# Order of the DMA queue and of three engine steps in the opening rounds of a linear-attention and expert kernel

## The chip, the cores and the metric

The kernel runs on one core of a Trainium2 chip. The metric is the device time of one execution in microseconds (us). A core has TensorE (matrix products), VectorE, ScalarE, GpSimd (POOL in the profile) and SyncE (SP), which here only issues transfers. Each engine runs its own queue of instructions in the order in which the program gives them, and an instruction that waits holds back all that is queued behind it on its engine. A transfer is issued by an engine's queue (nearly all of those below by SyncE's) and then runs on the core's 16 DMA engines.

## The reference

A linear attention with a decaying state feeds a mixture of experts whose gate is normalised over tokens and experts:

```python
# B=4, H=8, S=768, D=48; x has B*S = 3072 rows of H*D = 384; E = 8 experts, F = 1024
for t in range(S):
    cur = u * k[t] (outer) v[t]
    y[t] = r[t] @ (state + cur)
    state = w * state + k[t] (outer) v[t]
x = y as [3072, 384]
P = exp(x @ w_gate - max);  8 times: normalise rows, then columns
out = sum over e of P[:, e] * (relu(x @ w1[e]) @ w2[e])
```

All tensors are float32.

## The kernel before

**Tiles and rounds.** The 3072 tokens are 24 tiles of 128. The front of the kernel is a loop over rounds `i` (lines 791 to 850), software-pipelined over the tiles by a hand-written order: round `i` prepares tile `i+2`, turns tile `i+1`, forms the attention products of tile `i`, finishes the output of tile `i-1`, sends tile `i-2` through a transposing DMA and forms the gate logits of tile `i-3`. Expert 0's products are placed between these steps as units of work (`work`), from round 3 on; before that `work` issues three products of zeros as filler (`spin`, output `pz`). Behind the front, the other seven experts are computed in half-expert stages with a product scheme that uses combined tokens; this part is not changed.

**The steps**, each with the names under which the profile shows it:

- `load_part(tt, nm, src)` (line 314) loads r, k or v of a tile on SyncE (`rn`, `kn`, `vn`; tile 3's r and k go to a part of `hb`, those of tiles 4 and 5 to parts of `xv`). There are five buffers for v: tile `i+4` takes that of tile `i-1`. There are three buffers for r and k.
- `prep(tt)` (526): POOL multiplies r by a decay table (`rp`), VectorE does k (`kp`).
- `bonus_dot` and `bonus` (532, 541): POOL forms `rk` from r, k and u, VectorE reduces it to `dg`, POOL multiplies it into v and adds a term (`rk<-vn,dg`, `rk<-rk,hbx`).
- `stage_b(tt)` (551), the turn: eight TensorE transposes by products with the identity (`prT`, `pkT`), and ScalarE copies them out of PSUM (`rT`, `kT`).
- `stage_c(tt)` (562): the A products r by k (`pA`, 32 small matmuls), VectorE's masked copy (`at`), the state's products (`pu`), VectorE's and POOL's update of the state (`S`).
- `stage_d(tt)` (606): the output products (`py`), which are the last readers of the tile's v; VectorE sums (`x`), finds the largest value (`xm`) and a power-of-two scale (`inv_s`, `xs`).
- `scale_x(tt)` (639): ScalarE writes the high float16 part of the scaled x (`xsc`), VectorE the low part (also `xsc`).
- `stage_e(tt)` (646): SyncE issues the transposing DMA `hbx<-xsc`. Expert 0's products on this tile (`pht`, or `ph` from tile 3 on) and its gate logits (`px`, `stage_f`) read its result.
- `gate_across`, `gate_split` (511, 516): the scale and float16 split of the gate's weights (`pmax_wg`, `iswg`, `wgp`).

The PSUM pool of the attention products (`pa`) has four banks, taken in turn by prT, pkT, two of pA, pu and py.

**Expert 0's weights** are split into float16 high and low parts in small steps: `split_weights` (151) makes a list for w1 and then w2, each of three maxima on VectorE (`wm`), their maximum (`wma`), the maximum over partitions through TensorE (`pmax_w`), the scale (`isw`, `sw`), the high part's first half on ScalarE, the high part's second half with the low part's first half, and the low part's second half on VectorE (`ws`). `steps(n)` takes the next `n` of the list. How many each round takes, before and after `stage_d`, is the table `STEPS` (773). Two steps are taken ahead of the loop, three in round 0, so that round 1's two are w1's scale and the first half of its high part. The first `pht` product of round 3 needs w1's first halves, the first `po` product of round 6 those of w2.

**The order in the queues.** In rounds 2 to 19 the program issues r, k and v of tile `i+4` at the start of the round, and then `scale_x` and `stage_e` of tile `i-2`. In round 1, `stage_b(2)` comes ahead of `stage_c(1)`. Partial outputs of expert 0 are stored by SyncE too (`e0d<-stg`), and tokens of the later stages are copied by it (`xv<-hbx`).

Of the kernel before, what the change touches and what calls it, by code (L numbers as in the profile page):

```python
# [32 lines left out]
def rwkv_sinkhorn_moe(  # L33
# [24 lines left out]
    NTT = NT // P  # L58
# [27 lines left out]
    def part(home, dtype, at, shape):  # L86

        n = 1
        for s_ in shape:
            n *= s_  # L90
        x_ = home if home.dtype == dtype else home.bitcast(dtype)
        x_ = x_[:, at : at + n]
        if len(shape) == 1:
            return x_
        names = "abcd"[: len(shape)]
        return x_.rearrange(
            f"p ({' '.join(names)}) -> p {' '.join(names)}", **{c_: s_ for c_, s_ in zip(names[1:], shape[1:])}
        )
# [29 lines left out]
    def pow2_scale(m, inv, s, down):  # L128
        V.tensor_scalar(inv, m, 1e-30, down, op0=ALU.max, op1=ALU.mult)
        V.tensor_single_scalar(  # L130
            inv.bitcast(I32), inv.bitcast(I32), EXP_MASK, op=ALU.bitwise_and
        )
        V.reciprocal(s, inv)
# [144 lines left out]
    def whole(gen):  # L278
        leave()
        for _ in gen:  # L280
            pass
# [23 lines left out]
    def spin(n):  # L305
        pz = ps2.tile([P, TB], F32, tag="po", name="pz")
        for _ in range(n):
            T.matmul(pz, zeros[:, :P], zeros, start=True, stop=True)
# [5 lines left out]
    def load_part(tt, nm, src):  # L314
        b, c = divmod(tt, NCHB)
        if tt == 3 and nm != "v":
            t_ = part(hb3, F32, HB + "rk".index(nm) * H * D, (H, D))
        elif tt in (4, 5) and nm != "v":
            t_ = part(xv0_, F32, (2 * tt - 8 + "rk".index(nm)) * H * D, (H, D))
        else:  # L320
            t_ = ld.tile([P, H, D], F32, tag=nm + "n", name=f"{nm}n_{tt}", bufs=5 if nm == "v" else 3)
        Q.dma_start(t_, src[b, :, c * C : (c + 1) * C, :].rearrange("h t d -> t h d"))
        loads.setdefault(tt, {})[nm] = t_

    def load_chunk(tt):
        for nm, src in (("r", r), ("k", k), ("v", v)):
            load_part(tt, nm, src)
# [180 lines left out]
    def gate_max():  # L508
        V.tensor_reduce(wgm, wg, axis=AX.XY, op=ALU.max, apply_absolute_value=True)
# [16 lines left out]
    def prep(tt):  # L526
        ld_ = loads[tt]
        G.tensor_tensor(rp_[tt % 2][:, :, :D], ld_["r"], rt4, op=ALU.mult)
        V.tensor_tensor(kp_[tt % 3][:, :, :D], ld_["k"], kt4, op=ALU.mult)
        st[tt] = {}  # L530
# [20 lines left out]
    def stage_b(tt):  # L551
        d = st[tt]
        for nm, src in (("rT", rp_[tt % 2]), ("kT", kp_[tt % 3])):
            pt = ps3.tile([P, NPAIR, P], F32, tag="pa", name=f"p{nm}_{tt}")
            sv = src.rearrange("p (a j) d -> p a (j d)", j=2)
            for p_ in range(NPAIR):
                T.transpose(pt[:, p_, :], sv[:, p_, :], ident)
            dst = at2.tile([P, NPAIR, P], F32, tag=nm, name=f"{nm}_{tt}", bufs=3 if nm == "rT" else 2)
            S_.copy(dst, pt)
            d[nm] = dst  # L560
# [45 lines left out]
    def stage_d(tt):  # L606
        d = st[tt]
        c = tt % NCHB
        vn = loads[tt]["v"]
        at = at_[tt % 2]  # L610
        py = ps3.tile([P, H, D], F32, tag="pa", name=f"py_{tt}")
        pyp = py.rearrange("p (a j) d -> p a (j d)", j=2)

        halves = [slice(i * HP, (i + 1) * HP) for i in range(2)]
        first = True
        if c > 0:
            for p_ in range(NPAIR):
                for hs in halves:
                    T.matmul(
                        pyp[hs, p_, :], d["rT"][:, p_, hs], d["S"][:, p_].rearrange("p j d -> p (j d)"),  # L620
                        start=first, stop=False, skip_group_check=True,
                    )
                first = False
        for h in range(H):
            for hs in halves:
                T.matmul(
                    py[hs, h, :], at[:, h, hs], vn[:, h, :],
                    start=first, stop=(h == H - 1), skip_group_check=True,
                )
            first = False  # L630
        x = at2.tile([P, DM], F32, tag="x", name=f"x_{tt}")
        V.tensor_tensor(x, py.rearrange("p h d -> p (h d)"), d["av"].rearrange("p h d -> p (h d)"), op=ALU.add)
        m = at2.tile([P, 1], F32, tag="xm", name=f"xm_{tt}")
        V.tensor_reduce(m, x, axis=AX.X, op=ALU.max, apply_absolute_value=True)
        s = at2.tile([P, 1], F32, tag="xs", name=f"xs_{tt}")
        pow2_scale(m, inv_s[:, tt : tt + 1], s, 0.125)
        d["x"], d["s"] = x, s
# [97 lines left out]
    def token_steps(parts, sums=False):  # L735

        rebuild, singles, pool, high, low = parts
        steps = [[lambda th=th: rebuild(th)] for th in range(TH)]
        steps += [[f] for f in pool]
        if sums:  # L740
            return [lambda fs=fs: [f() for f in fs] for fs in steps]
        steps[2].append(singles)
        steps += [[], [], [], []]
        for (i, n), at_ in zip(PARTS, (5, 11, 15, 19)):
            steps[TH + at_].append(lambda i=i, n=n: high(i, n))
            steps[TH + at_ + 1].append(lambda i=i, n=n: low(i, n))
        return [lambda fs=fs: [f() for f in fs] for fs in steps]
# [6 lines left out]
    def prepare():  # L754
        if side and need.get(id(side[0]), 0) <= emitted[0]:
            side.pop(0)()

    def work(n, ready=True):
        if not ready:
            spin(3)  # L760
            return
        for _ in range(n):
            if units:
                whole(units.pop(0))
# [3 lines left out]
    for sg in range(3):  # L768
        steps = token_steps(early[sg], sg == 2)
# [1 line left out]
        side += steps  # L771

    STEPS = {
        0: (3, 0), 1: (0, 2), 2: (1, 1), 3: (2, 1), 4: (1, 0), 5: (1, 3), 6: (1, 0), 7: (0, 0), 8: (0, 0),
    }
    FIRST = TH

    def n_steps(i):
        return STEPS.get(i, (2, 2) if i < 22 else (3, 2))

    def steps(n):
        for _ in range(n):
            prepare()
# [7 lines left out]
    for i in range(NTT + 3):  # L791
        if i == 1:
            gate_max()
        if i + 2 < NTT:
            if i == 1:
                load_part(5, "v", v)
            elif 1 < i < NTT - 4:
                load_chunk(i + 4)
            if i:
                prep(i + 2)  # L800
        if i + 1 < NTT:
            bonus_dot(i + 1)
        if i + 1 < NTT and i:
            stage_b(i + 1)
        if 2 <= i <= NTT + 1:
            scale_x(i - 2)
            stage_e(i - 2)
            emitted[0] = i - 1
        work(1, i >= FIRST)
        if i < NTT:  # L810
            if i:
                bonus(i)
            if ("S", i) in st:
                st[i]["S"] = st.pop(("S", i))
            stage_c(i)
        if i == 0:
            fill(at_[1].rearrange("p h c -> p (h c)"))
            bonus(0)
            prep(2)
        if i == 2:  # L820
            gate_split(gate_res)
        if i == 0:
            stage_b(1)
        if i <= NTT:
            work(2 if i > 11 else 1, i >= FIRST)
        if i == 1:
            gate_res = gate_across()
        if i >= 3:
            bank_ = ps2.tile([P, TB], F32, tag="po", name=f"px_{i}")
        if i > NTT:  # L830
            work(2)
        steps(n_steps(i)[0])
        leave()
        if 1 <= i <= NTT:
            stage_d(i - 1)
        steps(n_steps(i)[1])
        if 3 <= i:
            stage_f(i - 3, bank_)
        done = i - 2
        if 0 <= done < TH:  # L840
            units += [g1_tile(done, j, W) for j in range(2)]
        if done == TH - 1:
            units += [g2_half(0, t, j, W) for j in range(2) for t in range(TH)]
        if TH <= done < NTT and done % TH == TH - 1:
            po_ = done // TH
            for j in range(2):
                g1 = [g1_unit(po_, fc, W) for fc in range(j * FHC, (j + 1) * FHC)]
                g2 = [g2_half(*a, W) for a in pend]
                units += merged(g1, g2)
                pend = [(po_, t, j) for t in range(TH)]  # L850
# [402 lines left out]
    for s in range(NS):  # L1253
        tasks = stage_tasks(s)
        for g in range(NG):
            for j in range(2):
                for n, nxt in enumerate(g1_slots(s, g, j)):
# [3 lines left out]
                    i = j * NPR + n  # L1261
# [37 lines left out]
```

## Time and profile before

| | |
|---|---|
| median of 3 runs | 1552.06 us (1550.48 to 1552.35) |
| profiled execution, own time | 1552.62 us |
| its span | 1551.1 us |
| TensorE busy | 1522.5 us, 98% |
| VectorE busy | 1026.8 us, 66% |
| ScalarE busy | 663.0 us, 43% |
| POOL busy | 596.2 us, 38% |
| front, rounds 0 to 26 | about the first 262 us |
| granted TensorE clock, mean | 0.993 |

Busy shares are means over stages with different limits, so the opening is read from the timeline, where each row has a start, a duration, the engine, the operation, its output and inputs, and in brackets the idle time of that engine just before, with what ended it. "SPq" is SyncE's queue: its rows are the issuing of a transfer, not the transfer. A busy TensorE is one whose pipeline holds products, at whatever clock; the granted clock is in the windows.

### The profile page before, as it was taken

What the parts mean: (1) busy time and instruction counts of PE and PEld (TensorE: products, weight loads), DVE (VectorE), ACT (ScalarE), POOL (GpSimd) and SP (SyncE); (2) the same over time, 40 slices, a digit from 0 to 9 for tenths busy, and PEclk for the clock granted to TensorE, in tenths of its full rate; (3) what the DMA queues carried; (4) which work ended last, traced back from release to release, by engine and by line L of the source; (5) the groups of instructions that cost most, each with busy time, mean ns of one, the idle gap of its engine ahead of it and who ended that gap; (6) DMA issues with size and microseconds to landing.
All of it is one profiled execution on the core that took longest, in us unless ns stands there. A gap on an engine that the chain in (4) does not pass through costs nothing.

```text
span 1551.1 us, 26486 instructions
## 1 busy us (share of the span) xinstructions
PE 1522.5 (98%) x10441; PEld 866.5 (56%) x10441; DVE 1026.8 (66%) x1715; ACT 663.0 (43%) x1164; POOL 596.2 (38%) x712
## 2 busy tenths in 40 slices
PE   7899999999999999999999999999999999999999
PEld 4766776555555555555555555555555555555555
DVE  7778885867665666766666666656566666656554
ACT  4233333524444453545444454535454444535320
POOL 7558995520202424242433424242423324242200
PEclk9899999999999999999999999999999999999999
DMA  8355533121226566576667566655545555545434
GB/s 193 61 113 108 127 83 104 49 77 50 97 58 109 73 122 95 72 124 93 126 87 129 79 122 90 124 69 86 65 59 97 60 97 60 97 56 100 54 90 134
DMA packets 186848, 143.14 MB, mean 92 GB/s; under 512 B 109537, under 2 KB 180961, under 8 KB 186721
## 3 DMA queue, kind: packets, MB, share of 16 engines
q0 software_dynamic: 44928, 61.36, 32.1%
q1 hardware_dynamic: 141584, 80.07, 18.8%
q8 instruction: 82, 1.34, 0.4%
q14 instruction: 46, 0.37, 0.1%
q10 hardware_dynamic: 208, 0.00, 0.0%
HBM read 55.39 MB, written 80.23 MB: 87 GB/s over the span
## 4 chain that ended last, share of the span: by engine, by line
PE 93%; DVE 4%; POOL 1%; issue 1%; DMA 1%; ACT 0%; SPq 0%; DVEq 0%; POOLq 0%; ACTq 0%
PE po L29 48%; PE bZ L29 12%; PE bY L29 12%; PE bA L29 5%; PE bB L29 5%; PE ph L29 4%; PE bC L29 2%; PE py L29 2%; PE pA L29 1%; PE pht L29 1%; DMA hbx<-xsc 1%; PE pz L29 1%; PE pu L29 1%; PE prT L29 0%; POOL rk L29 0%
## 5 line engine op out<-in xcount | busy, mean ns | idle before, releaser
L29 PE MATMUL po<-ws,hbx 128*128 128x384 f16 x3360 | 736.8, 326 | 0.0
L29 POOL DMA_DIRECT2D accd<-stg x288 | 250.4, 870 | 694.7 <-ACT stg L29 672.5
L29 PEld LDWEIGHTS <-hbx 128*128 128x128 f16 x3504 | 334.1, 98 | 292.6
L29 PEld LDWEIGHTS <-ws 128*128 128x128 f16 x3240 | 310.5, 99 | 249.7 <-issue 10.1
L29 ACT ACTIVATE hbx<-tb 128x512 f16<-128x512 f32 x224 | 141.0, 630 | 449.2 <-DVE tb L29 449.2
L29 PE MATMUL po<-ws,hb 128*128 128x384 f16 x1248 | 325.1, 328 | 5.9 <-ACT ws L29 2.5
L29 DVE TENSOR_TENSOR tb<-bY,tb 128x512 f32<-128x512 f32 x168 | 116.2, 692 | 195.7 <-PE bY L29 195.1
L29 ACT ACTIVATE stg<-po,pe 128x384 f32<-128x384 f32 x312 | 179.4, 575 | 122.7 <-PE po L29 97.1
L29 PE MATMUL bZ<-xv,ws 128*128 128x512 f16 x840 | 227.0, 379 | 0.4 <-DVE tb L29 0.4
L29 PE MATMUL bY<-xv,ws 128*128 128x512 f16 x840 | 227.0, 379 | 0.0
L29 DVE TENSOR_TENSOR tb<-bZ,tb 128x512 f32<-128x512 f32 x168 | 115.5, 688 | 136.1 <-PE bZ L29 136.0
L29 PEld LDWEIGHTS <-hb 128*128 128x128 f16 x1248 | 121.5, 98 | 100.3 <-issue 6.1
L29 POOL TENSOR_TENSOR ucb<-rawb 128x256 f32<-128x256 f32 x84 | 76.0, 955 | 115.0 <-DMA rawb<-in_moe_w_dram 115.0
L29 DVE TENSOR_TENSOR tb<-bB,tb 128x512 f32<-128x512 f32 x112 | 77.5, 692 | 49.1 <-PE bB L29 47.2
L29 DVE SCALAR_TENSOR_TENSOR hb<-tb,hbx 128x512 f16<-128x512 f32 x112 | 77.2, 690 | 24.6 <-ACT hbx L29 19.5
L29 PE MATMUL ph<-hbx,ws 128*128 128x384 f16 x504 | 91.5, 326 | 0.6 <-DVE hb L29 0.5
L29 PE MATMUL bB<-xv,ws 128*128 128x512 f16 x336 | 90.8, 379 | 0.0
L29 PE MATMUL bA<-xv,ws 128*128 128x512 f16 x336 | 90.8, 379 | 0.0
L29 DVE SCALAR_TENSOR_TENSOR hbx<-tb,hbx 128x512 f16<-128x512 f32 x112 | 77.6, 693 | 14.7 <-ACT hbx L29 10.4
L29 ACT COPY tb<-bZ 128x512 f32<-128x512 f32 x56 | 32.8, 586 | 65.5 <-PE bZ L29 65.5
L29 ACT COPY stg<-po 128x384 f32<-128x384 f32 x48 | 22.9, 477 | 69.9 <-PE po L29 62.4
L29 DVE SCALAR_TENSOR_TENSOR ws<-ucb,sw,ws 128x768 f16<-128x768 f32 (+1 forms) x56 | 51.8, 945 | 1.2 <-ACT ws L29 1.2
(174 smaller groups left out, 1533.3 us busy)
## 6 DMA issues: line engine op xcount, KB each, us to landing
accd<-stg POOLq DMA_DIRECT2D x288, 192.0 KB, 3.7
rawb<-in_moe_w_dram SPq DMA_DIRECT2D x28, 768.0 KB, 7.2
e0d<-stg SPq DMA_DIRECT2D x48, 192.0 KB, 1.9
hb<-e0d SPq DMA_DIRECT2D x48, 192.0 KB, 3.8
vn<-in_v_dram SPq DMA_DIRECT2D x24, 192.0 KB, 3.2
accd<-stg SPq DMA_DIRECT2D x24, 192.0 KB, 1.8
accd<-hb POOLq DMA_DIRECT2D x24, 192.0 KB, 4.8
rawb<-accd SPq DMA_DIRECT2D x24, 192.0 KB, 2.5
```

Of the source, the lines that this page charges most:

```text
L29: return lambda *a, **k: self.tc.keep_in_program_order(f(*a, **k))
```

## The change

Four edits in the order of the front's rounds; no instruction is added or removed, and none changes its size.

1. In rounds 2 to 19, r and k of tile `i+4` are issued behind the transposing DMA of tile `i-2` instead of ahead of it.
2. v of tile `i+4` is issued at the end of the round, behind `stage_d(i-1)`, also in round 1 (tile 5).
3. `stage_b(2)` in round 1 moves behind `stage_c(1)`. In round 0, `stage_b(1)` stood behind `stage_c(0)` already.
4. Of the steps on the weights, round 1 takes one instead of two at its end; the other, the first half of w1's high part on ScalarE, is taken in round 2 behind `scale_x(0)` and `stage_e(0)`.

```diff
     STEPS = {
-        0: (3, 0), 1: (0, 2), 2: (1, 1), 3: (2, 1), 4: (1, 0), 5: (1, 3), 6: (1, 0), 7: (0, 0), 8: (0, 0),
+        0: (3, 0), 1: (0, 1), 2: (1, 1), 3: (2, 1), 4: (1, 0), 5: (1, 3), 6: (1, 0), 7: (0, 0), 8: (0, 0),
     }
...
         if i + 2 < NTT:
-            if i == 1:
-                load_part(5, "v", v)
-            elif 1 < i < NTT - 4:
-                load_chunk(i + 4)
             if i:
                 prep(i + 2)
         if i + 1 < NTT:
             bonus_dot(i + 1)
-        if i + 1 < NTT and i:
+        if i + 1 < NTT and i > 1:
             stage_b(i + 1)
         if 2 <= i <= NTT + 1:
             scale_x(i - 2)
             stage_e(i - 2)
             emitted[0] = i - 1
+        if 1 < i < NTT - 4:
+            load_part(i + 4, "r", r)
+            load_part(i + 4, "k", k)
+        if i == 2:
+            steps(1)
         work(1, i >= FIRST)
...
-        if i == 0:
-            stage_b(1)
+        if i < 2:
+            stage_b(i + 1)
...
         if 1 <= i <= NTT:
             stage_d(i - 1)
+            if i + 4 < NTT:
+                load_part(i + 4, "v", v)
         steps(n_steps(i)[1])
```

## The prediction

> **What bounds the kernel now.** I read the windows first, then the order of time on TensorE, SyncE, VectorE and ScalarE. A windows row gives window and length, then busy time of PE, PEld, DVE, ACT and POOL with instruction counts, then granted TensorE clock, DMA share and GB/s.
>
> ```profile
> 20.80:76.00 55.20, 45.39 (x735) 39.53 (x736) 37.38 (x77) 14.54 (x23) 33.25 (x35) 0.85 0.47 101
> ...
> 400.00:500.00 100.00, 100.00 (x548) 53.44 (x547) 62.81 (x96) 45.66 (x81) 18.95 (x23) 1.00 0.38 91
> ```
>
> After the front, TensorE is busy for every microsecond: whatever the front gives, the rest starts earlier by that much and keeps it. In the 55.2 us of rounds 1 to 5 TensorE idles 9.8 us and runs at a granted clock of 0.85. The change can only pay there. The timeline (start, duration, engine, output<-inputs, then idle before it and its releaser) shows the idle time on TensorE:
>
> ```profile
> 19.68 0.27 PE L29 MATMUL pmax_w<-ident,wma 128*1 128x128 f32 x1 [2.31 <-DVE wma L29]
> 21.08 1.11 PE L29 MATMUL prT<-ident,rp 128*128 128x128 f32 x4 [1.12 <-POOL rp L29]
> ...
> 22.84 1.29 PE L29 MATMUL pz<-zeros 128*128 128x512 f16 x3
> 24.06 1.10 PE L29 MATMUL pA<-rT,kT 64*64 64x128 f32 x32
> ...
> 26.56 1.14 PE L29 MATMUL py<-vn,at 128*64 128x48 f32 x32
> ...
> 32.11 0.67 PE L29 MATMUL pu<-vn,kp 128*64 128x48 f32 x16 [1.41 <-ACT rT L29]
> ...
> 40.48 3.67 PE L29 MATMUL pht<-hbx,ws 128*128 128x128 f16 x36 [2.33 <-DMA hbx<-xsc]
> ...
> 54.19 3.72 PE L29 MATMUL pht<-hbx,ws 128*128 128x128 f16 x36 [3.31 <-DMA hbx<-xsc]
> ...
> 59.50 2.18 PE L29 MATMUL pht<-hbx,ws 128*128 128x128 f16 x36
> ...
> 67.06 3.01 PE L29 MATMUL pht<-hbx,ws 128*128 128x128 f16 x36 [2.49 <-DMA hbx<-xsc]
> 70.01 1.85 PE L29 MATMUL pA<-rT,kT 64*64 64x128 f32 x32
> ...
> 74.87 1.09 PE L29 MATMUL py<-vn,at 128*64 128x48 f32 x32
> ```
>
> Rounds 3, 4 and 5 each open with the first expert product (pht) waiting for the DMA transpose of x: 2.33, 3.31 and 2.49 us. Why is that transpose late? SyncE's queue and VectorE's making of its source answer it:
>
> ```profile
> 36.86 0.37 SPq L29 DMA_DIRECT2D vn<-in_v_dram  x1
> 37.43 1.34 SPq L29 DMA_TRANSPOSE hbx<-xsc  x1
> ...
> 49.81 0.37 SPq L29 DMA_DIRECT2D vn<-in_v_dram  x1
> 50.30 1.22 SPq L29 DMA_TRANSPOSE hbx<-xsc  x1
> ...
> 63.49 0.37 SPq L29 DMA_DIRECT2D vn<-in_v_dram  x1
> 63.96 1.22 SPq L29 DMA_TRANSPOSE hbx<-xsc  x1
> ```
>
> ```profile
> 29.89 0.76 DVE L29 TENSOR_TENSOR kp<-xv,ktab 128x384 f32<-128x384 f32 x1
> 33.10 0.62 DVE L29 SCALAR_TENSOR_TENSOR xsc<-x,xs,xsc 128x384 f16<-128x384 f32 x1 [2.44 <-ACT xsc L29]
> ...
> 37.34 1.80 DVE L29 SCALAR_TENSOR_TENSOR ws<-ws,sw,ws 128x1536 f16<-128x1536 f32 x1
> ...
> 43.77 0.61 DVE L29 SCALAR_TENSOR_TENSOR xsc<-x,xs,xsc 128x384 f16<-128x384 f32 x1
> ...
> 54.19 0.61 DVE L29 SCALAR_TENSOR_TENSOR xsc<-x,xs,xsc 128x384 f16<-128x384 f32 x1
> ```
>
> The sources are complete at 33.7, 44.4 and 54.8; the transposes go out at 37.4, 50.3 and 64.0, each right behind a v load. That load takes the buffer of tile i-1, free only when the round's last products (py) end. So 3.7, 5.9 and 9.2 us of each transpose's delay are queueing on SyncE.
>
> **The change, part by part.** Times are in the profiled execution (span 1551.1 us, own time 1552.62, which is 0.56 above the median 1552.06).
>
> *Tile 2's turn behind the A products (round 1).* TensorE ends pmax_w at 19.95, then waits 1.12 us for POOL's rp and does the turn (21.08 to the filler's start at 22.84, 1.76 us) before pA. Now filler (0.8 to 1.29 us, the row above) and pA come first: pA at about 20.8, and the turn fills the place behind pu, when rp has long been there. py of tile 0 starts at 26.56 - (24.06 - 20.8) + 1.76 = 25.1, a gain of 1.5. Ends: 3.3 (were the turn free) and 0 (were pA to wait for something not shown).
>
> *w1's first high part behind x's (round 2).* ScalarE's queue shows what it stood ahead of:
>
> ```profile
> 30.01 1.58 ACT L29 ACTIVATE ws<-ws,sw 128x1536 f16<-128x1536 f32 x1 [6.29 <-DVE sw L29]
> 31.50 0.57 ACT L29 COPY rT<-prT 128x512 f32<-128x512 f32 x1
> 31.96 0.59 ACT L29 COPY kT<-pkT 128x512 f32<-128x512 f32 x1
> 32.44 0.62 ACT L29 ACTIVATE xsc<-x,xs 128x384 f16<-128x384 f32 x1
> ```
>
> ScalarE sat idle 6.29 us for the scale, and rT, kT and x's high part queued behind 1.58 us of weights. Moved, rT goes at about 27.1 (its products 1.5 earlier, no wait), kT ends at 28.3, x's high part at 28.9. VectorE's low part of x then follows kp directly: 30.65 - 1.5 = 29.2 instead of 33.10. The moved 1.58 us is covered: it runs at 28.9 to 30.5, and its reader, VectorE's ws low part, comes 4.2 us after the xsc row (37.34 against 33.10), so at 33.4. Without that cover it would cost at most 1.58.
>
> *The transpose ahead of the loads.* In round 3 the transpose is issued at 29.8 and needs some 3.1 us (63.96 to 67.06). The DMA engines are still full then:
>
> ```profile
> 28.00:30.00 2.00, 2.00 (x27) 1.45 (x30) 1.79 (x9) 0.00 (x0) 1.92 (x3) 1.00 1.04 223
> 30.00:32.00 2.00, 0.71 (x28) 0.47 (x20) 0.65 (x1) 1.99 (x3) 1.43 (x2) 1.00 0.93 176
> 32.00:34.00 2.00, 1.89 (x27) 1.28 (x28) 0.90 (x2) 1.06 (x3) 0.00 (x0) 1.00 0.62 124
> 34.00:36.00 2.00, 2.00 (x38) 2.00 (x36) 1.97 (x5) 0.00 (x0) 1.67 (x2) 0.51 0.00 0
> ```
>
> They empty before 34, so it lands between 32.9 and about 34.5. Late next is ws's low part: 33.4 + 1.8 = 35.2. Round 3's pht starts at about 35.3 instead of 40.48: 5.2 gained so far. For rounds 4 and 5, VectorE's work moves by 3.9 as a whole (33.10 to 29.2). The second transpose's source is complete at 44.4 - 3.9 = 40.5, so it lands at 43.6; TensorE gets there at 54.19 - 3.31 - 5.2 = 45.7, and the 3.31 us go. The third lands at 54.8 - 3.9 + 3.1 = 54.0; TensorE gets there at 67.06 - 2.49 - 5.2 - 3.3 - 1.5 (the clock, below) = 54.6, and the 2.49 go. Ends for the two: 5.8, and 0 if VectorE falls behind by as much.
>
> *The clock.* The first pht of a round costs 3.67, 3.72, 3.01 us where the second costs 2.18; after the waits TensorE runs slow, and pA at 70.01 takes 1.85 against 1.10. With the waits of rounds 4 and 5 gone I take 1.54 + 0.83 + 0.75 = 3.1 us; ends 0 and, with round 3's 1.49, 4.6. I keep round 3 slow, since the 0.51 clock at 34 to 36 follows a gap of only 1.41 us. The Trainium skill's page "TensorE: Matmul & The Clock Gate", Part 1, says that the clock halves after an idle window of about 3.4 us and returns after a busy one. By that rule alone round 3's would be fast as well and the sum 1.5 better; the 0.51 row here disagrees about the length of the gap, so the row decides.
>
> *v at the round's end; r and k behind the transpose.* v was issued there already, by its wait (36.86, 49.81, 63.49): 0. r and k go out after x's low part instead of a round's start, for tiles used two rounds later: 0, covered by that distance of over 20 us; exposed, each costs its landing, 3.5 us. In later rounds SyncE waits for POOL with its r and k loads anyway, which come behind the transpose now:
>
> ```profile
> SPq L29 <- POOL rk L29: 43.7, 11, 6.2
> ```
>
> *Sum.* 5.2 + 3.3 + 2.5 + 3.1 = 14.1 us for the products of tile 4 (74.87) and what follows. VectorE must keep up. Its busy time from x's first low part to the scale of w2:
>
> ```profile
> 33.10:55.27 22.17, 16.53 (x255) 14.90 (x256) 20.85 (x38) 6.24 (x10) 14.89 (x14) 0.83 0.42 76
> 55.27:78.25 22.98, 19.68 (x340) 17.97 (x339) 12.32 (x30) 4.08 (x7) 10.24 (x12) 0.87 0.23 46
> ```
>
> 29.2 + 20.85 + 12.32 = 62.4 at the soonest, against 78.25 - 14.1 = 64.2 asked: 1.8 us of room in 33. Too little for nothing to collide, and these rows show the price of collisions between VectorE and POOL:
>
> ```profile
> 37.45 2.54 POOL L29 TENSOR_TENSOR rp<-xv,rtab 128x384 f32<-128x384 f32 x1
> ...
> 53.73 0.55 DVE L29 TENSOR_TENSOR kp<-kn,ktab 128x384 f32<-128x384 f32 x1
> ...
> 65.29 1.29 DVE L29 TENSOR_TENSOR kp<-kn,ktab 128x384 f32<-128x384 f32 x1
> ```
>
> kp takes 0.74 more where POOL runs beside it; rp beside ws's low part 2.54, where 1.0 is usual. I allow three kp-sized collisions, 2.1 us: 14.1 - 2.1 = 12.0. From round 6 on everything moves as a block, the wait for w2's low part included:
>
> ```profile
> 81.75 3.63 PE L29 MATMUL po<-ws,hb 128*128 128x384 f16 x11 [1.53 <-DVE ws L29]
> ```
>
> So 1552.06 - 12.0 = 1540.1 us.
>
> **Rivals.**
> *A: VectorE and POOL become the bound.* The stretch shrinks to 41 to 43 us with 37.38 of VectorE and 33.25 of POOL in it. If rounds 3, 4 and 5 each pay kp's 0.74 and rp's 1.54, 6.8 of 14.1 is lost: 7.3 gained, 1544.8. For it: both rows. Against: POOL has 22 us idle there now. The Trainium skill's "SBUF — State Buffer", section "Who interferes with whom", says that a VectorE instruction with two SBUF inputs and a GpSimd one that reads SBUF block each other for a whole instruction. The 2.54 row agrees, and by that rule alone this rival would be the likelier.
> *B: the transposes stay late.* If they land only behind the load backlog, or the low parts of w1 hold them anyway, only round 1 and 2's 1.5 to 3.9 remain: 1549. Against: the 3.7 to 9.2 us between source and issue.
> *C: slower.* SyncE now stands still at each transpose until x's low part, with r, k and the partial outputs' stores behind it. Were stores held so that each of rounds 6 to 23 lost over 12.0 / 18 = 0.67 us, the gain would be gone; at 1 us, 1558. Against: before, the same stores stood behind v, which waited longer, to the round's end.
> *D: more.* All clocks fast, no collision: 14.1 + 1.5, 1536.5.
>
> **Chances.** Forecast (1538 to 1543) 0.68, A 0.18, B 0.06, C 0.03, D 0.05. A change within 0.2% (3.1 us) is about what a measurement of this kernel cannot tell from none. Faster: forecast, A, D and a part of B, 0.92; same 0.05; slower 0.03. The range 1537 to 1546 takes the forecast, A and the edge of D.
>
> **What would show it.** In the changed profile: transposes right behind xsc, none behind a v load; no pht waiting for hbx in rounds 4 and 5; round 3's pht at about 35 with ws's low part as releaser; rT of tile 3 near 27; pA of tile 1 near 21; py of tile 4 near 62 to 63; first and second pht of a round alike in rounds 4 and 5. It would be wrong if TensorE then waits as long for VectorE's at, x or hb, or if later rounds show new waits for stg or for r and k.

## The result and the profile after

The changed kernel takes 1541.18 us (median of 4 runs, 1539.44 to 1541.45) against 1551.77 us for the kernel before (4 runs, 1550.48 to 1552.35) on the same chip: 10.6 us less, ratio 0.9931 with a 95% interval of 0.9913 to 0.9948. Forecast were 1540.1 us and 12.0 us less. The profiled execution of the changed kernel took 1541.45 us and has a span of 1539.9, 11.2 less than the span before.

The timeline of TensorE after the change, rows that stand opposite to those shown of before:

```profile
20.61 0.37 PE L29 MATMUL pmax_w<-ident,wma 128*1 128x128 f32 x1 [3.32 <-DVE wma L29]
20.77 1.49 PE L29 MATMUL pz<-zeros 128*128 128x512 f16 x3
22.19 1.99 PE L29 MATMUL pA<-rT,kT 64*64 64x128 f32 x32
...
27.51 1.14 PE L29 MATMUL py<-vn,at 128*64 128x48 f32 x32
...
35.91 0.27 PE L29 MATMUL pht<-hbx,ws 128*128 128x128 f16 x2
37.95 2.07 PE L29 MATMUL pht<-hbx,ws 128*128 128x128 f16 x34 [1.76 <-DVE ws L29]
...
47.69 2.17 PE L29 MATMUL pht<-hbx,ws 128*128 128x128 f16 x36 [1.02 <-DMA hbx<-xsc]
...
56.35 2.17 PE L29 MATMUL pht<-hbx,ws 128*128 128x128 f16 x36
58.45 1.10 PE L29 MATMUL pA<-rT,kT 64*64 64x128 f32 x32
...
62.83 0.27 PE L29 MATMUL pmax_w<-ident,wma 128*1 128x128 f32 x1 [1.16 <-DVE hb L29]
...
63.74 1.09 PE L29 MATMUL py<-vn,at 128*64 128x48 f32 x32
...
70.62 3.56 PE L29 MATMUL po<-ws,hb 128*128 128x384 f16 x11 [1.53 <-DVE ws L29]
```

Of 2.33, 3.31 and 2.49 us of waiting for the transpose, 1.02 in round 4 is left. Round 3 now waits 1.76 for the weights' low part instead, as foreseen. Round 5 does not wait. New is the 1.16 for VectorE's hb behind round 5. From there all is a block: py of tile 4 is 11.13 sooner than before, po 11.13, the end 11.2.

SyncE's queue and VectorE's making of the transposes' sources, after:

```profile
32.53 1.34 SPq L29 DMA_TRANSPOSE hbx<-xsc  x1
...
35.26 0.64 SPq L29 DMA_DIRECT2D vn<-in_v_dram  x1
43.22 1.22 SPq L29 DMA_TRANSPOSE hbx<-xsc  x1
...
53.09 1.22 SPq L29 DMA_TRANSPOSE hbx<-xsc  x1
```

```profile
18.67 0.56 DVE L29 TENSOR_TENSOR kp<-kn,ktab 128x384 f32<-128x384 f32 x1 [0.92 <-DMA kn<-in_k_dram]
...
31.85 0.61 DVE L29 SCALAR_TENSOR_TENSOR xsc<-x,xs,xsc 128x384 f16<-128x384 f32 x1
...
36.09 1.81 DVE L29 SCALAR_TENSOR_TENSOR ws<-ws,sw,ws 128x1536 f16<-128x1536 f32 x1
...
42.54 0.61 DVE L29 SCALAR_TENSOR_TENSOR xsc<-x,xs,xsc 128x384 f16<-128x384 f32 x1
...
52.40 0.61 DVE L29 SCALAR_TENSOR_TENSOR xsc<-x,xs,xsc 128x384 f16<-128x384 f32 x1
...
59.12 1.28 DVE L29 SCALAR_TENSOR_TENSOR xsc<-x,xs,xsc 128x384 f16<-128x384 f32 x1
```

Each transpose now goes out within 0.1 us of the end of its source (32.46, 43.15, 53.01), where 3.7 to 9.2 us lay between. The sources themselves are only 1.2 to 1.8 us sooner than before. The windows of the changed kernel, in the columns used above:

```profile
20.00:26.00 6.00, 5.39 (x56) 3.80 (x57) 4.01 (x11) 0.00 (x0) 5.84 (x7) 0.50 1.06 231
...
20.00:76.00 56.00, 47.44 (x813) 39.02 (x814) 44.74 (x97) 19.19 (x29) 38.76 (x41) 0.91 0.55 121
```

TensorE does 813 products up to 76 us, where it did 735 before. The first row shows what the forecast had not seen: a granted clock of 0.50 for six microseconds, behind a gap of 3.32 us. In the same window the kernel before has 0.72, behind a gap of 2.31.

### The profile page after: what moved, and what is told of

Same layout as the page of the kernel before. It is cut to its first block, busy times and chain, and to the rows that moved or that the text cites. A ratio compares the mean times of both kernels' runs of the same rounds, so it can differ in the third digit from the quotient of the medians.

```text
span 1539.9 us, 26490 instructions
## 1 busy us (share of the span) xinstructions
PE 1516.7 (98%) x10441; PEld 861.4 (56%) x10441; DVE 1026.4 (67%) x1715; ACT 662.1 (43%) x1164; POOL 594.9 (39%) x712
## 4 chain that ended last, share of the span: by engine, by line
PE 93%; DVE 5%; POOL 1%; SPq 1%; DMA 0%; issue 0%; ACT 0%; POOLq 0%; DVEq 0%
PE po L29 48%; PE bZ L29 12%; PE bY L29 12%; PE bA L29 5%; PE bB L29 5%; PE ph L29 4%; PE bC L29 2%; PE py L29 2%; PE pA L29 1%; SPq L29 1%; PE pu L29 1%; DVE ws L29 1%; PE prT L29 0%; DMA kn<-in_k_dram 0%; DVE hb L29 0%; PE pkT L29 0%
## 5 line engine op out<-in xcount | busy, mean ns | idle before, releaser
L29 PEld LDWEIGHTS <-ws 128*128 128x128 f16 x3240 | 307.1, 98 | 244.2 <-issue 2.7
```

Of the source, the lines that this page charges most:

```text
L29: return lambda *a, **k: self.tc.keep_in_program_order(f(*a, **k))
```

## The experiments

There are four groups: the table's four kernels, the next four, the three with the filler in other kernels, and the three fillers. Each group was timed beside its own runs of the kernel before, whose medians were 1551.78, 1551.52, 1551.26 and 1551.03 us. Differences from the kernel before are taken within a group.

**The loads' order alone, the steps' order alone, and the wait without the order.** The theory: v waits for its buffer on SyncE, and the transpose stands behind it. If so, a sixth buffer for v must do what the new order does.

The kernel before with the loads' part of the change only:

```diff
-            if i == 1:
-                load_part(5, "v", v)
-            elif 1 < i < NTT - 4:
-                load_chunk(i + 4)
...
+        if 1 < i < NTT - 4:
+            load_part(i + 4, "r", r)
+            load_part(i + 4, "k", k)
...
+            if i + 4 < NTT:
+                load_part(i + 4, "v", v)
```

> The kernel before with the order of the loads alone changed (transpose ahead of r and k, v at the round's end); tile 2's turn and w1's high part stay where they were. Theory Q (the transpose queues behind v's buffer): pht of round 3 waits for w1's low part, at about 39.2 instead of 40.5, and the waits of rounds 4 and 5 for the transpose (3.3 and 2.5 us) go with their slow first products: 8 to 10 us faster. Theory E (the gain comes from the two engine steps that moved): under 3 us faster, with new waits for VectorE in place of the old ones.

The kernel before with the turn's and w1's part only:

```diff
-        0: (3, 0), 1: (0, 2),
+        0: (3, 0), 1: (0, 1),
...
-        if i + 1 < NTT and i:
+        if i + 1 < NTT and i > 1:
...
+        if i == 2:
+            steps(1)
...
-        if i == 0:
-            stage_b(1)
+        if i < 2:
+            stage_b(i + 1)
```

> The kernel before with the two engine steps alone moved (tile 2's turn behind the A products, w1's first high part behind x's); the loads stay where they were. Theory Q: x's low part comes 1 to 4 us sooner, but the transpose still goes out behind v, so only what the py of each round gains is passed on: 1.5 to 2.5 us faster, and TensorE still waits 2 to 3.5 us for the transpose in each of rounds 3, 4 and 5. Theory E: 7 us faster or more.

The kernel before, its order untouched, with six buffers for v and (for room) one for x:

```diff
-  bufs=5 if nm == "v" else 3
+  bufs=6 if nm == "v" else 3
...
-  tag="x", name=f"x_{tt}")
+  tag="x", name=f"x_{tt}", bufs=1)
```

> The kernel before in its own order, with a sixth buffer for v (x has one buffer instead of two to make room), so that the v load ahead of the transpose finds its buffer free and doesn't wait for the round's py. Theory Q: the transposes go out right behind x's low part although nothing was reordered, and the time is that of the kernel with only the loads reordered, 8 to 10 us faster, within 1.5 us of it. If it is the order itself that counts (r and k ahead of the transpose fill the DMA engines or SyncE), the transposes stay over 2 us behind x's low part and under 5 us are gained.

And the changed kernel again, beside the same runs of the kernel before:

> The changed kernel itself, on this chip, for the comparison with its parts: 10 to 11.5 us faster than before. If the parts add up, the gains of the loads alone and of the steps alone sum to this within 2 us.

| kernel | median (runs) | against before | ratio (95%) |
|---|---|---|---|
| loads only | 1543.56 (1543.14 to 1544.57) | -8.2 | 0.9950 (0.9937 to 0.9964) |
| steps only | 1549.12 (1548.49 to 1550.33) | -2.7 | 0.9985 (0.9976 to 0.9994) |
| six v buffers | 1543.57 (1542.19 to 1545.01) | -8.2 | 0.9948 (0.9935 to 0.9962) |
| the change again | 1541.02 (1540.42 to 1541.50) | -10.8 | 0.9933 (0.9919 to 0.9946) |

SyncE's queue with six v buffers, in the old order, then TensorE's first products of rounds 4 and 5 there:

```profile
32.83 0.71 SPq L29 DMA_DIRECT2D vn<-in_v_dram  x1
34.37 1.34 SPq L29 DMA_TRANSPOSE hbx<-xsc  x1
```

```profile
49.66 2.17 PE L29 MATMUL pht<-hbx,ws 128*128 128x128 f16 x36
...
58.31 2.17 PE L29 MATMUL pht<-hbx,ws 128*128 128x128 f16 x36
```

And with the steps alone, where three waits of 2.5 to 3.2 us stay and the second source, ready at 42.48, goes out at 47.81 behind v. (The third wait is put down to VectorE's xsc by the profile; the transpose issued at 59.79 landed 3.0 us later, 0.15 ahead of its end.)

```profile
47.32 0.37 SPq L29 DMA_DIRECT2D vn<-in_v_dram  x1
47.81 1.22 SPq L29 DMA_TRANSPOSE hbx<-xsc  x1
```

```profile
38.01 2.80 PE L29 MATMUL pht<-hbx,ws 128*128 128x128 f16 x36 [2.61 <-DMA hbx<-xsc]
...
51.58 2.17 PE L29 MATMUL pht<-hbx,ws 128*128 128x128 f16 x36 [3.21 <-DMA hbx<-xsc]
...
62.94 3.75 PE L29 MATMUL pht<-hbx,ws 128*128 128x128 f16 x36 [2.53 <-DVE xsc L29]
```

So the cause is shown: with six buffers v is still issued ahead of the transpose and does no harm, because its buffer is free. The buffer and the order are worth the same 8.2 us, and the parts add up (8.2 + 2.7 = 10.9 against 10.8).

**The two small edits, taken back one at a time from the changed kernel.** Turn back (`if i + 1 < NTT and i:` and `if i == 0: stage_b(1)`):

> The changed kernel with tile 2's turn put back ahead of the A products of round 1. By the prediction's term it loses 1.5 us (9.2 faster than before instead of 10.7). By the traces of the parts, where TensorE does the same list of work ahead of py either way and waits only 0.1 us for rp, it loses 0 to 0.5 us.

w1's first high part back in round 1 (`1: (0, 2)`, no `steps(1)` in round 2):

> The changed kernel with the first half of w1's high part put back into round 1, ahead of rT, kT and x's high part on ScalarE. By the prediction's term x's low part comes 2.4 us later and the whole loses about that (8.2 to 8.6 faster than before). If the turn's move is what brought x forward, it loses under 1 us. If the transposes' order has made VectorE the bound so that ScalarE no longer matters, it loses nothing.

Turn back: 1542.29 us (1542.00 to 1542.87), 9.2 less than before. w1 back: 1542.81 us (1541.13 to 1543.82), 8.7 less. The change gained 10.6 and 10.8 against its own runs of before, so the turn's place is worth 1.4 to 1.5 us and w1's 1.9 to 2.1, where 2.4 was expected. For w1 the reason is that of the prediction. VectorE waits for ScalarE again:

```profile
33.70 0.62 DVE L29 SCALAR_TENSOR_TENSOR xsc<-x,xs,xsc 128x384 f16<-128x384 f32 x1 [2.15 <-ACT xsc L29]
```

For the turn it isn't: with it back, py of tile 0 starts no later (26.78, against 26.85 in the change run again). The wait for rp, 1.12 in the profile of before, is 0.22 here:

```profile
20.99 0.66 PE L29 MATMUL prT<-ident,rp 128*128 128x128 f32 x4 [0.22 <-POOL rp L29]
21.48 0.99 PE L29 MATMUL pkT<-ident,kp 128*128 128x128 f32 x4
22.26 1.49 PE L29 MATMUL pz<-zeros 128*128 128x512 f16 x3
23.68 1.70 PE L29 MATMUL pA<-rT,kT 64*64 64x128 f32 x32
...
26.78 1.14 PE L29 MATMUL py<-vn,at 128*64 128x48 f32 x32
...
37.66 2.97 PE L29 MATMUL pht<-hbx,ws 128*128 128x128 f16 x34 [2.05 <-DVE ws L29]
```

The last row shows one difference: round 3's pht at 2.97 where the change has 2.07, and pA behind it at 1.80 instead of 1.10. But round 4 takes that back, since here it does not wait for its transpose: py of tile 4 starts at 63.44, against 63.13 and 63.74 in the two profiles of the change. In these profiles the loss opens only in round 6, behind the same wait of 1.53 for w2's low part. There po takes 3.68 instead of 3.49 and 3.56, and pA is slow; turn back first, then the change:

```profile
73.93 1.99 PE L29 MATMUL pA<-rT,kT 64*64 64x128 f32 x32
```

```profile
74.12 1.11 PE L29 MATMUL pA<-rT,kT 64*64 64x128 f32 x32
```

So the turn's 1.4 to 1.5 us has the size of the prediction's term, but did not come by its path. Why the clock there stays low for longer is open.

**The clock ahead of pA.** If the gap ahead of pmax_w and the half clock behind it ate the turn's gain, products of zeros in that gap must bring it back. The changed kernel with 13 instead of 3 of them at the end of round 0 (`spin(3)` becomes `spin(n)`, 13 there and 3 elsewhere):

> The changed kernel with 13 instead of 3 filler products at the end of round 0, which fill most of TensorE's 3.3 us of idle time ahead of pmax_w. If that gap is what slows TensorE's clock in round 1 (pA 1.99 us, filler 1.49), pA takes 1.10 and filler 0.81, py of tile 0 comes 1.5 to 2.5 us sooner and 1 to 2.5 us are gained on the changed kernel. If round 1 is bound by the loads or by VectorE instead, the products are fast and wait, and nothing is gained.

1539.54 us (1539.23 to 1540.92), 12.0 less than before, where the change alone gained 10.6 and 10.8. pA takes 1.10, and py of tile 0 comes at 24.43. Then the same filler in the kernel before, in the changed kernel with the turn back, and once more in the changed kernel, measured together:

> The kernel before, with 13 instead of 3 products of zeros at the end of round 0, nothing else. Theory 1 (the filler's gain is the clock's alone and reaches the end only where nothing else holds round 3): py of tile 0 comes about 1.3 us sooner than 26.56 (pA and pu at 1.10 and 0.67 or less, the turn unchanged), but x's low part still waits for ScalarE's first half of w1, and the transposes still stand behind v, whose buffer comes free with py: the front gains at most that 1.3 us, so 1550.5, not told from no change. Theory 2 (the filler's gain is independent of the order of SyncE's queue): the 1.5 us that it gave to the changed kernel, 1550.2, with v's loads, the transposes and the three waits each earlier by 1.5. Both would be wrong if the time fell by 3 us or more.

> The changed kernel with 13 products of zeros at the end of round 0 and with tile 2's turn back ahead of tile 1's A products. Theory 1 (the turn's move was worth 1.5 us as predicted, and the slow clock after the 3.3 us gap ate it): with the clock kept, py of tile 0 comes 0.8 to 1.5 us later than the 24.43 of the kernel with the filler alone (the filler now stands behind the turn, and a wait for rp ahead of it), and the time is 1540.5 to 1541. Theory 2 (the turn's place is worth nothing, because the same products run either way and rp is there in time): py at 24.4 and the time that of the kernel with the filler alone, 1539.5.

> The changed kernel with 13 products of zeros at the end of round 0, once more, beside the other two on the same chip. Both theories: 1539.5 (1539.0 to 1541), py of tile 0 at about 24.4.

They took 1550.07 (1548.11 to 1552.12; ratio 0.9992, 0.9983 to 1.0001), 1541.05 (1540.02 to 1541.79) and 1539.60 (1538.64 to 1540.97). Turn back, with the filler:

```profile
21.15 0.66 PE L29 MATMUL prT<-ident,rp 128*128 128x128 f32 x4 [1.12 <-POOL rp L29]
...
25.32 1.14 PE L29 MATMUL py<-vn,at 128*64 128x48 f32 x32
```

Turn behind pA as in the change, with the filler, and the window that had a clock of 0.50:

```profile
20.90 1.10 PE L29 MATMUL pA<-rT,kT 64*64 64x128 f32 x32
...
24.37 1.14 PE L29 MATMUL py<-vn,at 128*64 128x48 f32 x32
```

```profile
20.00:26.00 6.00, 5.95 (x100) 4.45 (x101) 4.66 (x12) 1.14 (x2) 5.84 (x7) 1.00 1.06 235
```

With the clock kept, the turn's move is worth 0.95 us at py, where the prediction had 1.5, and 1.45 us in the medians (the ranges of the two kernels overlap). From pmax_w to py the profiles show it in all kernels: without the filler 6.45 to 6.90 with the turn behind and 6.28 to 6.97 with it ahead, so nothing; with the filler 4.28 to 4.32 behind, 4.65 and 5.56 ahead. The 5.56 holds a wait of 1.12 for rp, the 4.65 (the kernel before with the filler) one of 0.21: most of the turn's worth is that wait. In the kernel before, py comes 1.55 sooner with the filler, but the time only falls by 1.2 us, which isn't told from nothing and doesn't separate the two theories. There the transposes still wait for v, as its round 4 shows.

```profile
51.04 3.64 PE L29 MATMUL pht<-hbx,ws 128*128 128x128 f16 x36 [3.21 <-DMA hbx<-xsc]
```

**What is left in the front.** First, w2's split earlier in the changed kernel (`3: (2, 2), 4: (1, 0), 5: (3, 0)`), against the 4 us at round 6's po:

> The changed kernel with the steps on w2 taken earlier: the maximum in round 3, the one over partitions in round 4, scale and the first three splits of round 5 ahead of stage_d instead of behind it. It aims at the 4 us that TensorE still idles at the start of round 6 for w2's high and low parts. If those parts are late only by their place in the order, the wait goes and 3 to 5.5 us are gained on the changed kernel (with the slow clock behind it). If VectorE is the bound there, the low part delays x and the products wait for that instead: under 1.5 us gained.

1540.75 us (1540.33 to 1542.97), not told from the change. In its profile (1542.97, the longest of its runs) po's waits of 2.46 for the high part and 1.53 for the low part shrink to none and 0.84, but pmax_w, now in round 4, waits 2.93 for VectorE's hb and round 5's second pht 1.99 more: the wait moved to VectorE.

Then fillers in the two gaps left, 8 products of zeros ahead of round 3's pht and 11 ahead of round 6's po, beside the 13:

```diff
+        if i in (3, 6):
+            spin({3: 8, 6: 11}[i])
         work(1 if i >= FIRST else 3, i >= FIRST)
```

> The kernel with the 13 products of zeros at the end of round 0, and with 8 more products of zeros ahead of round 3's first pht and 11 ahead of round 6's first po, in both of the gaps that are left for the weights' low parts. Theory 1 (what is left in the front is the clock behind those two gaps): with the clock kept, round 3's pht takes 2.2 instead of 2.9 to 3.6 and pA 1.1 instead of 1.9, 1.5 us; round 6's eleven po products take 2.0 instead of 3.68, 1.7 us; the waits themselves stay. VectorE and POOL give back about half of round 3's part, so 1539.6 - 0.8 - 1.7 = 1537.1. Theory 2 (the clock there stays slow, because a gap of 1.5 us for the low part still stands behind the filler, or the gain is taken back by a later wait for VectorE): 1539.5, as with the one filler.

1538.04 us (1537.74 to 1538.96), ratio 0.9916 (0.9902 to 0.9930): 13.0 less than before, and its longest run is below every run of the changed kernel. Its TensorE and its window:

```profile
36.40 2.07 PE L29 MATMUL pht<-hbx,ws 128*128 128x128 f16 x34 [0.82 <-DVE ws L29]
...
69.75 1.95 PE L29 MATMUL po<-ws,hb 128*128 128x384 f16 x11 [1.53 <-DVE ws L29]
```

```profile
20.00:76.00 56.00, 51.07 (x862) 40.38 (x862) 48.96 (x100) 19.71 (x30) 40.25 (x42) 1.00 0.56 123
```

The wait of 1.53 stands, but the eleven po products behind it take 1.95 instead of 3.56. That is the first theory, though its gain of 1.5 to 1.6 us over the medians of the one filler (1.0 to 1.3 against each group's kernel before) is well short of the 2.5 that it expected.

## Why the prediction was right, and where its terms were off

The leads over before, from the rows above, beside the prediction's:

| place | predicted | measured |
|---|---|---|
| py of tile 0 | 1.5 | -0.95 |
| x's first low part | 3.9 | 1.25 |
| round 3's pht, start | 5.2 | 2.53 for all but the first two products |
| round 3's pht, end | 5.2 | 4.13 |
| round 4's pht, start | 8.5 | 6.50 |
| round 5's pht, start | 12.5 | 10.71 |
| py of tile 4 | 12.0 | 11.13 |
| end of the span | 12.0 | 11.2 |

**The transposes behind v: right.** The three waits were queueing on SyncE: the new order and the sixth buffer each take them away alone. As named, round 3's pht then waits for ws's low part and round 5's for nothing; round 4's is the exception, below.

**"py of tile 0 starts at ... 25.1, a gain of 1.5": wrong, the step that failed.** It summed the moved products at full clock (filler 0.8, pA 1.10). They ran at 0.50: 1.49 and 1.99, then pu 1.09. So two of the signs that were named failed, pA of tile 1 near 21 (22.19) and rT of tile 3 near 27 (29.58). Besides, this profile's kp of tile 2 waits 0.92 for its load, and pmax_w starts at 20.61. In the other profiles pmax_w lies at 19.76 to 20.89, so the 19.68 of before was its early end, and the rp wait of 1.12, on which the term rested, is there only where pmax_w is early. Of the ends given, 3.3 and 0, the lower one is what the runs show without the filler; with it they show 0.95.

**w1's high part: right.** Without VectorE's wait for ScalarE, x's low part comes 2.5 us sooner, where 2.4 was meant (33.70 with w1 back and 31.19 in the change run again; loads only 33.63, steps only 31.18). In time it is worth 1.9 to 2.1. The 1.58 us moved are covered as said: they end at 32.63 in the changed kernel, and VectorE's ws low part starts at 36.09.

**Round 3 "slow": wrong by 1.6, in favour.** pht took 2.07 and the lead grew from 2.53 to 4.13. The prediction took the slow case from one row, a gap of 1.41 us ahead of a slow stretch. Behind a gap of 1.40 us in the same place the loads-only kernel ran fast; the kernel before first, then loads only:

```profile
34.89 1.90 PE L29 MATMUL py<-vn,at 128*64 128x48 f32 x32
```

```profile
35.02 1.09 PE L29 MATMUL py<-vn,at 128*64 128x48 f32 x32
```

So that row could not decide it. Nor do the runs give a rule by which it had to be fast: round 3's pht was slow in ten of the fourteen profiles (see the end).

**Round 4's 3.31 "go": 2.29 did.** Its source was complete at 43.15, not 40.5, late by the 2.65 us that x's first low part fell short (3.9 against 1.25), and its transpose took 4.3 us to land where the others took 2.5 to 2.6. This view of the tile gives the spread:

```profile
DMA to landing us min/median/max: 2.5/2.6/4.3
```

With 2.6 it would have landed at 45.8, ahead of TensorE's 46.67. Among the kernels in which it goes out right behind its source, that landing took 4.1 to 4.6 in four profiles (the change twice, w2's split, the first filler) and 2.5 to 2.8 in seven (loads only, six v buffers, turn back, w1 back, turn back with the filler, the filler again, three fillers). What held it is open.

**The clock in rounds 4 and 5, "3.1": measured.** 3.72 to 2.17, 3.01 to 2.17, 1.85 to 1.10: 1.55 + 0.84 + 0.75 = 3.14.

**The allowance of 2.1 for VectorE and POOL: 1.2.** It is the 1.16 at pmax_w for hb, behind an xsc of 1.28 beside POOL instead of 0.61. So rival A was there at a sixth of its 6.8 us. In the filler's kernel only a part of the 2.4 us gained at py reaches the end (1.2 to 1.5 in the times). In its first profile, round 3 waits 2.40 in all (1.26 for the transpose, 1.14 for the low part) instead of 1.76, and pht behind it runs slow at 3.57. VectorE's first xsc and ws take 1.36 and 2.20 beside POOL there, instead of 0.61 and 1.81, which is rival A again.

**The rivals.** B fell: the transposes go out behind their sources, and the loads alone gain 8.2. C fell: later rounds lose nothing, as the lead of 11.13 at py of tile 4 is 11.2 at the end. D fell with the half clock in round 1 and the 1.02 and 1.16 that stayed.

Added up from the table's steps: 2.53 + 1.60 + 2.29 + 1.55 + 2.49 + 0.25 (small rows of rounds 3 and 4) + 0.84 + 0.75 - 1.16 = 11.1, of 11.2 in the span. The forecast was near in part by luck, because its errors offset each other: 2.7 us too much ahead of round 3's pht and 1.0 too much for round 4's transpose, against 1.6 too little for round 3's clock, 0.9 too much set aside for VectorE and POOL, and the 0.25 of small rows. The mechanism of the transposes, which carries 8.2 of the 10.8 us, is not luck.

## What to carry to other kernels

A transfer that is late may be neither slow nor late in its source: look at what stands ahead of it in its issuing queue, and at whether that waits for a buffer. Here a new order and one more buffer were worth the same 8.2 us. Cost moved products at the clock of the place they move to, and ask of each wait in a single profile whether it comes from a load's chance arrival.

## What the runs showed of the hardware

Products of zeros in a gap pay although they compute nothing. Where TensorE idled 3.2 to 3.4 us ahead of pmax_w, pA took 1.70 to 1.99 (granted clock 0.50 in the changed kernel's window from 20 to 26 us), and with the filler 1.10 (1.00). With three such fillers the gain over the kernel before is 13.0 us instead of 10.8.

How long a gap must be is not settled. Counted from the turn to the bulk of its products, round 3's pht had 1.59 us of idle time (w2's split) and 1.76 (the change, twice) and ran at full clock. It ran slow behind 2.05 to 2.64 us in ten profiles (turn back 2.05, the kernel before with the filler 2.64). But the length alone doesn't decide. Behind 3.21 us round 4's pht ran at full clock in the steps-only kernel (2.17) and slow in the kernel before with the filler (3.64). Behind 1.41 us the kernel before ran slow in round 2 (py 1.90), and behind 1.40 four others ran at full clock there (1.09: loads only, six v buffers, w1 back, the kernel before with the filler).

The Trainium skill's "TensorE: Matmul & The Clock Gate", Part 1, lets the clock halve after an idle window of about 3.4 us. All these gaps are shorter, so by that rule alone none of them would have slowed the clock, and the measurement decides. That page also calls the window free-running, so that the outcome depends on the phase. The two spreads at nearly one length are of that kind; no run here shows the window itself.
